# A cap on bulk weight loads in flight, and Wo loaded in four pieces, in a fused attention and MLP block

## The chip, the cores and the metric

The kernel runs on one core of one Trainium2 chip. A core has TensorE (PE, matmuls), VectorE (DVE), ScalarE (ACT, activation functions), GpSimd (POOL) and SyncE (SP), which here only issues DMAs. Each engine runs its own instructions in order and waits on semaphores for the others. The metric is the device time of one execution in microseconds (us); the median of three runs counts.

## The reference

One transformer block in bfloat16 for 2048 tokens: layer norm, attention with 32 heads of 32, an output projection with a residual, layer norm, and an MLP with tanh-GELU and a second residual.

```python
# x [1, 2048, 1024]; wqkv [1024, 3072]; wo [1024, 1024]; w1 [1024, 3584]; w2 [3584, 1024]
def A(x):                       # H = 32, Dh = 32
    q, k, v = heads(x @ wqkv)
    p = softmax(q @ k.T * Dh ** -0.5)
    return merge(p @ v) @ wo
def B(x):
    return gelu_tanh(x @ w1 + b1) @ w2 + b2
h = x + A(layernorm(x))
out = h + B(layernorm(h))       # layernorm: (x - mean) / sqrt(var + 1e-5), no weights
```

## The kernel before

**Order by a planner.** The kernel does not write its instructions down directly. `Graph.add` (L96) records tasks with their engine, an assumed duration, a priority, and the tasks that they depend on, found from the buffers that each reads and writes. `Graph.schedule` (L119) then plays the whole program through in simulated time and fixes the order of each engine's tasks. On SP it takes, of the tasks that are ready, the one of lowest priority number, and of these the one recorded first. It counts on 280 GB/s for all DMAs together, one after the other, and a fixed latency of 2.1 us. There are 24 lanes, a semaphore each, for DMAs in flight; a DMA waits for the one before it on its lane. `assign` (L229) turns dependencies into semaphore waits, and `emit` (L322) writes the order out. So an edit of the planner's DMA rules can move matmuls and vector work too: the order on all engines follows from its simulated times. On the chip that order is fixed, and only the semaphores decide when each instruction runs.

**Stages.** Norm, transposes and the first projections start the kernel (about 25 us). From then on attention runs as 512 rounds: a group of eight score matmuls (`Att.qk`, L805) writes two units of two PSUM banks, and two exponentials of 128 x 1024 (L816) empty them into PT or, at the start, PX buffers. PV matmuls (L842) and softmax sums (L857 on DVE, L871 on PE) follow. Three units of PSUM rotate, so ScalarE is at most one exponential ahead of the next group of scores. A unit of queries is 256 tokens, u = 0 to 7. Between the score groups the planner fits the remaining TensorE work in ("bg"): projections, and for each unit u the output projection `wo(u)`, the norm `ln2(u)`, `ffn1(u)` and `ffn2(u, j)` for the two halves j of the output columns. For unit 7 these can only follow the last exponential: they form a serial end. `pick_pe` prefers scores, and it may put idle matmuls ("keep") where nothing else is ready in two stretches (`KEEP`).

**Weights.** `block_copies` (L909) first rewrites Wo, W1 and W2 in HBM as contiguous blocks of 512 KB (Wo: two of 1 MB), at priority 3. After that every unit loads all of them again, since they don't fit beside the attention buffers. SBUF has a ring of four 512 KB slots for W1 (`a_w1r`) and one of seven for W2 (`a_w2r`); unit 7's FFN1 and FFN2's second half have rings of their own where K and V lay (`b_w1r`, `b_w2r`, which share their space). Wo (`wov`, two tensors of 1 MB) lies over the four W1 slots: `wo(u)` needs slots 0 and 1 for its first 1 MB and slots 2 and 3 for its second. All these loads have priority 1. A load is issued when its slot's last reader is done, so the loads for the next unit's first half of W2 go out as soon as slots come free, far ahead of their use, and there is no limit on how many are in flight.

Other DMAs on SP's queue: query tiles QT (64 KB, priority -1), query scratch writes, residual rows `hch`, output rows, and the DMA transposes of the normed rows (`hnT`, priority -1), on which FFN1 depends.

Names in the profile: `w_blocks` and `wo_blocks` are the HBM blocks, `gT` the MLP's hidden layer, `OT` attention's output, `uu` the GELU's temporary (its Tanh is L1023). All DMAs carry L589, the matmul helper L565 (four narrow tiles) and L568 or L571 (one whole).

Of the kernel before, what the change touches and what calls it, by code (L numbers as in the profile page):

```python
# [10 lines left out]
E = mybir.EngineType  # L11

P = 128
# [4 lines left out]
KEEP = ((262, 298), (930, 1010),)  # L18
KEEP_COLS = 512
KEEP_GAP = -0.08  # L20


class Buf:
# [42 lines left out]
class Graph:  # L66
# [47 lines left out]
    def schedule(self, pick_pe, pool, switch=0.104, dma_rate=280.0, dma_lat=2.1, dma_issue=0.06):  # L114
# [9 lines left out]
        state = {"mode": None, "dma": 0.0}  # L124
        events = []
        n = 0
        num = {t: i for i, t in enumerate(self.tasks)}

        def release(t):
# [16 lines left out]
        while n < total:  # L146
# [5 lines left out]
            now = heapq.heappop(events)  # L152
            while events and events[0] <= now + 1e-9:
                heapq.heappop(events)
            for e in self.ENGS:
                while free[e] <= now + 1e-9:
                    up = upcoming[e]
                    rd = ready[e]
# [4 lines left out]
                    if e == E.PE:  # L163
                        state["next"] = up[0][0] if up else None
                        t = pick_pe(rd, now, state, free_banks(now))
                    else:
                        t = min(rd, key=lambda x: (x.prio, num[x]))
                        if up and t.prio > 0:

                            for (rt, _, u) in up[:6]:  # L170
                                if u.prio < t.prio and rt < now + 0.6 * t.occ:
                                    t = None
                                    break
# [3 lines left out]
                    if t.acq is not None:  # L177
                        b = min([x for x in free_banks(now) if x in t.acq.banks], key=lambda x: max([y.done for y in pool[x]], default=0.0))
# [8 lines left out]
                    t.order = len(seqs[e])  # L187
                    seqs[e].append(t)
                    if e == E.SP:
                        k = min(range(self.n_lanes), key=lambda i: lanes[i].done if lanes[i] else 0.0)  # L190
                        if lanes[k] is not None:
                            t.deps.add(lanes[k])
                            start = max(start, lanes[k].done)
                        lanes[k] = t
                        t.lane = k
                        free[e] = start + dma_issue
                        s0 = max(state["dma"], start + 0.9)
                        state["dma"] = s0 + t.bytes / dma_rate / 1e3
                        t.done = max(state["dma"], s0) + dma_lat - 0.9
                    else:  # L200
                        free[e] = start + t.occ
                        t.done = start + t.occ + t.lat
# [135 lines left out]
def build_kernel(nc, A_x, A_wqkv, A_wo, B_w1, B_b1, B_w2, B_b2, out):  # L338
# [7 lines left out]
    DC = D // P  # L346
# [237 lines left out]
    def dma(out_ap, in_ap, nbytes, reads=(), writes=(), prio=0, noncontig=False, after=()):  # L584
        def fn(s):
            if noncontig:
                with nc.allow_non_contiguous_dma(reason="strided gather"):
                    return s.dma_start(out_ap, in_ap)
            return s.dma_start(out_ap, in_ap)  # L589
        return gr.add(E.SP, fn, 0.06, 0.0, reads, writes, prio, nbytes=nbytes, after=after)  # L590
# [350 lines left out]
    def wo(u, tail=False):  # L941
        R = R1
        nb = 0
        R.cnt["w1"] += -R.cnt["w1"] % 4
        for j in range(2):
            dma(wov[j][:, :, :], wod[j], P * DC * 1024, reads=[B_wod[j]], writes=R.B_w1[2 * j:2 * j + 2], prio=1)
        R.cnt["w1"] += 4
        for t in range(2):
            hs = 2 * (u % 2) + t
# [2 lines left out]
            for j in range(2):  # L952
# [4 lines left out]
                order = range(G) if tail else [7, 0, 1, 2, 3, 4, 5, 6]  # L957
                for k, g in enumerate(order):
                    mm(bank, OT[:, u % 3, g, t * P:(t + 1) * P], wov[j][:, g, :], k == 0, k == 7 and not tail,
                       [B_OT[u % 3][g][t], R.B_w1[s], R.B_w1[s + 1]], not tail)  # L960
                if tail:
                    mm(bank, ident[:, :], hch[:, hs, c], False, True, [B_ident, B_hch[hs][j]], False)
                    act(lambda a, hs=hs, c=c, bank=bank: a.activation(hch[:, hs, c], psum[:, bank, :], ACT.Copy), 512,
# [63 lines left out]
    def ffn2(u, j, wide=False, W=None, banks=None):  # L1027
# [3 lines left out]
        ws = []  # L1031
        for q in range(FC // 4):
            s = W.next("w2", W.nw2)
            dma(W.w2[:, s, :, :], w2d[j, q], P * 4096, reads=[B_w2d[j][q]], writes=[W.B_w2[s]], prio=1)
            ws.append(s)
        for t in range(2):
            bank = banks[t] if banks and banks[t] is not None else slot()
# [302 lines left out]
```

## Time and profile before

| | |
|---|---|
| median of three runs | 1080.27 us (1079.21 to 1081.98) |
| the profiled execution | 1079.06 us |
| its span, first to last instruction | 1077.3 us, at full granted TensorE clock |
| DMA engines | moved 196.37 MB, 182 GB/s on average; busy for 54.0% with the data queue, 0.9% with the "instruction" queue |
| W2 blocks `a_w2r` | 105 loads of 512 KB, median 5.2 us from issue to landing |
| W1 blocks `a_w1r` | 98 loads of 512 KB, 3.5 us |
| Wo `wov` | 16 loads of 1 MB, 4.8 us |
| DMA transposes `hnT` | 14, median 3.2 us |

A line of a group names the source line, the engine, the operation, what it writes and reads, and how often; then its busy time, the mean of one in ns, and the engine's idle time just before it with what ended most of that. A line of the chain or of the timeline has the start in us, the duration, the engine or line, and how many instructions are merged; a bracket tells idle time before it and what ended it. A line of the waits has the waiting engine and line, whom it waited for, and total us, times, longest. An exponential lasts longer (1084 ns in the median) than the distance between two, since ScalarE overlaps them.

### The profile page before, as it was taken

Reading aid. Unit: us, or ns where it says so; the run is one execution under the profiler, and the core shown is the slowest. Engines: PE = TensorE matmul, PEld = TensorE weight load, DVE = VectorE, ACT = ScalarE, POOL = GpSimd, SP = SyncE. Lnnn points to the kernel's source line nnn. Section 1 sums busy time; section 2 is a strip of 40 time slices with the busy share of each in tenths; the row PEclk is TensorE's granted clock in tenths of the full one; section 3 lists DMA queues with packets and bytes.
Section 4 is the critical chain, followed back from the end, with each engine's and each line's share of the span. In section 5 each row is a group of like instructions: output and inputs, shape, how many; then the busy total and the mean of one; then the engine's idle time right before and its main releaser. Section 6 shows DMA issues by size and latency. Waiting matters only on the chain.

```text
span 1077.3 us, 41835 instructions
## 1 busy us (share of the span) xinstructions
PE 1053.3 (98%) x19071; PEld 609.4 (57%) x19071; DVE 747.3 (69%) x1438; ACT 1013.3 (94%) x1116; POOL 45.4 (4%) x110
## 2 busy tenths in 40 slices
PE   8999999999999999999999999999999999999998
PEld 6576555554444754674475457447545754575483
DVE  8776666566576895698489659948975976696401
ACT  4999999999999999999999999999999999999650
POOL 4200000000010000001000100100010000000100
PEclk9999999999999999999999999999999999999999
DMA  8561543438473555655664764466375555866260
GB/s 223 166 172 30 159 134 119 138 119 297 165 186 130 188 191 181 232 181 169 217 240 164 209 230 179 154 223 230 144 232 205 186 200 181 294 220 250 94 244 19
DMA packets 136177, 196.37 MB, mean 182 GB/s; under 512 B 49216, under 2 KB 100288, under 8 KB 133184
## 3 DMA queue, kind: packets, MB, share of 16 engines
q1 hardware_dynamic: 136000, 193.70, 54.0%
q8 instruction: 149, 2.44, 0.9%
q14 instruction: 28, 0.23, 0.1%
HBM read 177.94 MB, written 27.26 MB: 190 GB/s over the span
## 4 chain that ended last, share of the span: by engine, by line
ACT 60%; PE 33%; DVE 4%; POOL 1%; issue 1%; DMA 0%; SPq 0%; POOLq 0%; DVEq 0%
ACT PT L816 55%; PE ps L568 11%; PE ps L565 7%; PE ps L571 5%; PE ps L805 5%; PE ps L842 3%; ACT PX L816 3%; ACT uu L1023 2%; PE ps L871 2%; DVE PS L857 1%; DVE st L617 1%; DMA xrb<-in_A_x_dram 0%; DVE gT L1001 0%; DVE gT L1025 0%; POOL denb L626 0%
## 5 line engine op out<-in xcount | busy, mean ns | idle before, releaser
L816 ACT ACTIVATE PT<-ps 128x1024 bf16<-128x1024 f32 x992 | 922.0, 1094 | 5.9 <-PE ps L805 5.7
L857 DVE TENSOR_TENSOR PS<-PT 128x1024 bf16<-128x1024 bf16 x431 | 285.3, 685 | 132.4 <-PE ps L871 67.6
L805 PE MATMUL ps<-QT,KT 32*128 32x256 bf16 x4096 | 203.9, 273 | 5.6 <-ACT PT L816 2.7
L842 PE MATMUL ps<-PT,V 128*32 128x256 bf16 x3968 | 174.2, 273 | 2.1 <-ACT PT L816 1.7
L805 PEld LDWEIGHTS ps<-QT,KT 32*128 32x128 bf16 x4096 | 61.0, 92 | 161.4 <-ACT PT L816 135.9
L871 PE MATMUL ps<-PS,ones 128*32 128x256 bf16 x1756 | 122.0, 274 | 2.3 <-DVE PS L857 1.2
L842 PEld LDWEIGHTS ps<-PT,V 128*32 128x32 bf16 x3968 | 101.7, 97 | 28.5 <-issue 7.0
L568 PE MATMUL ps<-hnT,a_w1r 128*128 128x256 bf16 x940 | 114.5, 273 | 0.6 <-DVE gT L1001 0.5
L565 PE MATMUL ps<-a_w2r,gT 128*32 128x512 bf16 x1436 | 102.2, 381 | 0.1
L568 PEld LDWEIGHTS ps<-hnT,a_w1r 128*128 128x128 bf16 x940 | 86.8, 98 | 24.4 <-issue 13.7
L568 PE MATMUL ps<-a_w2r,gT 128*128 128x512 bf16 x397 | 97.6, 381 | 0.8 <-DVE hch L966 0.6
L565 PE MATMUL ps<-hnT,a_w1r 128*32 128x256 bf16 x2512 | 89.8, 274 | 3.5 <-DVE OD L894 1.5
L1001 DVE TENSOR_TENSOR gT<-ps,b1f 128x512 bf16<-128x512 f32 x98 | 67.3, 686 | 16.0 <-PE ps L568 8.0
L565 PEld LDWEIGHTS ps<-hnT,a_w1r 128*32 128x32 bf16 x2512 | 61.8, 96 | 19.5 <-issue 16.5
L1046 DVE SCALAR_TENSOR_TENSOR hch<-ps,hch 128x512 bf16<-128x512 f32 x32 | 21.9, 685 | 70.5 <-PE ps L571 47.1
L871 PEld LDWEIGHTS ps<-PS,ones 128*32 128x32 bf16 x1756 | 46.2, 96 | 26.6 <-DVE PS L857 8.6
L568 PEld LDWEIGHTS ps<-a_w2r,gT 128*128 128x128 bf16 x397 | 33.7, 98 | 46.5 <-issue 13.0
L568 PE MATMUL ps<-xnT,Wall 128*128 128x512 bf16 (+1 forms) x272 | 57.4, 346 | 0.4 <-ACT xnT L645 0.2
L1023 ACT ACTIVATE uu<-uu 128x1024 bf16<-128x1024 bf16 x49 | 54.3, 1113 | 0.0
L565 PEld LDWEIGHTS ps<-a_w2r,gT 128*32 128x32 bf16 x1436 | 32.0, 96 | 25.4 <-issue 13.5
L622 POOL CAST mvb<-mv 128x2 bf16<-128x2 f32 (+1 forms) x25 | 5.2, 216 | 972.5 <-DVE mv L619 972.5
L568 PE MATMUL ps<-wov,OT 128*128 128x512 bf16 x146 | 35.4, 380 | 1.4 <-DVE OD L894 0.8
(93 smaller groups left out, 1020.8 us busy)
## 6 DMA issues: line engine op xcount, KB each, us to landing
a_w2r<-w_blocks SPq DMA_DIRECT2D x105, 512.0 KB, 5.2
a_w1r<-w_blocks SPq DMA_DIRECT2D x98, 512.0 KB, 3.5
wov<-wo_blocks SPq DMA_DIRECT2D x16, 1024.0 KB, 4.8
w_blocks<-in_B_w_dram SPq DMA_DIRECT2D x28, 512.0 KB, 3.9
b_w1r<-w_blocks SPq DMA_DIRECT2D x14, 512.0 KB, 3.9
a_w1r<-in_A_wqkv_dram SPq DMA_DIRECT2D x11, 512.0 KB, 5.5
Wall<-in_A_wqkv_dram SPq DMA_DIRECT2D x17, 256.0 KB, 4.9
xrb<-in_A_x_dram SPq DMA_DIRECT2D x16, 256.0 KB, 4.7
```

What stands on the lines that cost most here:

```text
L565: fns.append(lambda p, j=j: p.matmul(psum[32 * j:32 * j + 32, bi(bank), c0:c1], lhsT[:, 32 * j:32 * j + 32], rhs, start=start, stop=stop, ...
L568: t.whole = lambda p: p.matmul(psum[:, bi(bank), c0:c1], lhsT, rhs, start=start, stop=stop, skip_group_check=True)
L571: t = pe(lambda p: p.matmul(psum[:, bi(bank), c0:c1], lhsT, rhs, start=start, stop=stop), occ, reads=reads, writes=[bb(bank)], mode="full" ...
L617: dve(lambda v, c=c, k=k, x_ap=x_ap: v.bn_stats(st_l[:, i + k, 6 * c:6 * c + 6], x_ap[:, 512 * c:512 * c + 512]), 0.595, reads=B_x if isin ...
L805: return p.matmul(psum[:, 2 * us[h // 2] + h % 2, 256 * i:256 * i + 256], KT[32 * h:32 * h + 32, g, k0:k0 + P], QT[32 * h:32 * h + 32, qs, :],
L816: act(lambda a, u=u, k=k: a.activation(PTs[s][:, k, :, :], psum[:, 2 * u:2 * u + 2, :], ACT.Exp, bias=0.0, scale=SCALE), 1024, reads=[B_ps ...
L842: fns.append(lambda p, i=i, h=h: p.matmul(psum[32 * h:32 * h + 32, bi(bank), 0:256], V[:, g, 2 * r + i, 32 * h:32 * h + 32], PTs[s][:, h / ...
L857: dve(lambda v: v.tensor_tensor(PS[:, n, :, :], pairs[:, :, 0:256], pairs[:, :, 256:512], ALU.add), c_dve(1024, 2), reads=B_PTs[s], writes ...
L871: fns.append(lambda p, h=h, rhs=rhs, i=i: p.matmul(psum[32 * h:32 * h + 32, bi(bank), 256:512], ones32[:, :], rhs, start=False, stop=last, ...
L1001: t = dve(lambda v: v.tensor_tensor(g[:, fc:fc + 2, :], psum[:, bi(bank), :].rearrange("p (f c) -> p f c", f=2), b1f[:, fc:fc + 2].unsquee ...
L1023: act(lambda a: a.activation(w, w, ACT.Tanh, bias=0.0, scale=KT2), 1024, reads=[B_uu[i]], writes=[B_uu[i]], prio=-1)
L1046: drop(dve(lambda v, hs=hs, bank=bank, half=half: v.scalar_tensor_tensor(hch[:, hs, c], psum[:, bi(bank), :], half, hch[:, hs, c], ALU.mul ...
```

## The change

- The planner keeps a list of bulk loads: DMAs of 512 KB or more with priority 1 or 2. Such a load may be issued only when the loads before it that are still out, with itself, are no more than three units of 512 KB (priority 1) or two (priority 2). The wait for the earlier landing becomes a semaphore wait in the program.
- For bulk loads the planner counts on 350 GB/s instead of 280.
- The first half of W2 (j = 0) has priority 2 instead of 1: where both are ready, W1, Wo and the second half of W2 go first.
- Wo comes in four loads of 512 KB instead of two of 1 MB, each into one W1 slot, and each Wo matmul waits only for the piece that it reads.

The writes of normed rows to scratch early in the kernel (1 MB, priority 1) fall under the limit too; the HBM-to-HBM copies (priority 3) and the reloads of Wqkv (priority 0 and below) don't.

```diff
+BULK = {1: 3, 2: 2}
+UNIT = 1 << 19
...
+        bulk = []
+
+        def behind(t):
+            k = BULK[t.prio] - t.bytes // UNIT
+            for b in reversed(bulk):
+                k -= b.bytes // UNIT
+                if k < 0:
+                    return b
+            return None
...
-                        t = min(rd, key=lambda x: (x.prio, num[x]))
+                        go = rd
+                        if e == E.SP:
+                            go = []
+                            for x in rd:
+                                b = behind(x) if x.bytes >= UNIT and x.prio in BULK else None
+                                if b is None or b.done <= now + 1e-9:
+                                    go.append(x)
+                                else:
+                                    heapq.heappush(events, b.done)
+                            if not go:
+                                break
+                        t = min(go, key=lambda x: (x.prio, num[x]))
...
+                        if t.bytes >= UNIT and t.prio in BULK:
+                            b = behind(t)
+                            if b is not None:
+                                t.deps.add(b)
+                            bulk.append(t)
...
-                        state["dma"] = s0 + t.bytes / dma_rate / 1e3
+                        state["dma"] = s0 + t.bytes / (350.0 if t.bytes >= UNIT and t.prio in BULK else dma_rate) / 1e3
...
         for j in range(2):
-            dma(wov[j][:, :, :], wod[j], P * DC * 1024, reads=[B_wod[j]], writes=R.B_w1[2 * j:2 * j + 2], prio=1)
+            for i in range(2):
+                dma(wov[j][:, 4 * i:4 * i + 4, :], wod[j][:, 4 * i:4 * i + 4, :], P * DC * 512, reads=[B_wod[j]],
+                    writes=[R.B_w1[2 * j + i]], prio=1)
...
-                       [B_OT[u % 3][g][t], R.B_w1[s], R.B_w1[s + 1]], not tail)
+                       [B_OT[u % 3][g][t], R.B_w1[s + g // 4]], not tail)
...
-            dma(W.w2[:, s, :, :], w2d[j, q], P * 4096, reads=[B_w2d[j][q]], writes=[W.B_w2[s]], prio=1)
+            dma(W.w2[:, s, :, :], w2d[j, q], P * 4096, reads=[B_w2d[j][q]], writes=[W.B_w2[s]], prio=2 if j == 0 else 1)
```

In the built program SP issues 480 DMAs instead of 464. TensorE's score matmuls, and the work of DVE, ACT and POOL, keep their number; their order among each other changes in many places between the start and the last exponential. The narrow and whole forms of the other matmuls are mixed a little differently, and there are 31 idle matmuls instead of 24.

## The prediction

> **What bounds the kernel now.** I read the page first: busy shares, the costliest groups, the DMA issues.
>
> ```profile
> span 1077.3 us, 41835 instructions
> ...
> PE 1053.3 (98%) x19071; PEld 609.4 (57%) x19071; DVE 747.3 (69%) x1438; ACT 1013.3 (94%) x1116; POOL 45.4 (4%) x110
> ...
> L816 ACT ACTIVATE PT<-ps 128x1024 bf16<-128x1024 f32 x992 | 922.0, 1094 | 5.9 <-PE ps L805 5.7
> ...
> a_w2r<-w_blocks SPq DMA_DIRECT2D x105, 512.0 KB, 5.2
> a_w1r<-w_blocks SPq DMA_DIRECT2D x98, 512.0 KB, 3.5
> wov<-wo_blocks SPq DMA_DIRECT2D x16, 1024.0 KB, 4.8
> ```
>
> TensorE and ScalarE are both nearly full, so the question is which sets the pace. The chain of waits, in order of time, shows long runs of exponentials (L816) back to back:
>
> ```profile
> 64.09 251.43 ACT PT L816 x274
> ...
> 492.41 57.00 ACT PT L816 x62
> 549.41 0.94 ACT uu L1023
> ```
>
> 251.43 / 274 = 0.9176 us for one exponential when nothing holds it up; a Tanh (L1023) is 0.94. Line 816 has 1024 executions (992 into PT, 32 into PX), two of them before 21.82 us. From the start of the third at 21.82 to the start of the last at 1009.69 there are 987.87 us. The work in them is 1021 x 0.9176 + 49 x 0.94 = 982.9. So ScalarE loses 4.9 us in 988, and this is all that a change between these two points can win. The list of waits agrees:
>
> ```profile
> ACT PT L816 <- PE ps L805: 5.7, 8, 3.0
> ```
>
> Eight gaps make 5.7 us, and the longest, 3.0, lies in the start-up before 21.82; the other seven make 2.7, and the rest of the 4.9 is slips too short to be listed. I looked at the seven in the timeline. The largest two are like this one, at 425 us:
>
> ```profile
> 424.77 0.28 PE L805 MATMUL ps<-QT,KT 32*128 32x256 bf16 x1
> ...
> 425.54 0.39 PE L805 MATMUL ps<-QT,KT 32*128 32x256 bf16 x7 [0.49 <-issue]
> ...
> 425.98 1.94 ACT L816 ACTIVATE PT<-ps 128x1024 bf16<-128x1024 f32 x2 [0.62 <-PE ps L805]
> ```
>
> TensorE stops inside a group of score matmuls, waiting for nothing that the profile shows, and the next exponential starts 0.62 late (0.77 of delay, so the reserve here is 0.15). Four of the seven are of this kind: 0.62, 0.26, 0.19 and 0.82 us of ScalarE idle at 425, 738, 808 and 925, together 1.89. In all four a 16 KB packet of the queue that the page calls "instruction" starts 2.2 to 2.3 us before the stall ends; I take them for code that arrives late, an inference. The other three (0.16, 0.44, 0.18 at 362, 757, 907) are places where TensorE had more work than the exponentials gave it time for. None of the seven waits for a weight load. The load with the least time to spare is Wo's second megabyte:
>
> ```profile
> 485.47 0.32 SPq L589 DMA_DIRECT2D wov<-wo_blocks  x1
> ...
> 492.00 1.25 PE L568 MATMUL ps<-wov,OT 128*128 128x512 bf16 x5
> ```
>
> It lands 4.7 us after its issue, at 490.15, and its first matmul starts at 492.00: 1.85 to spare.
>
> After the last exponential comes a serial end: the last Wo, its norm, FFN1 and FFN2.
>
> ```profile
> 1025.57 24.63 PE L571 MATMUL ps<-hnT,b_w1r 128*128 128x256 bf16 x224
> 1027.52 10.80 SPq L589 DMA_DIRECT2D b_w2r<-w_blocks  x7
> 1050.03 12.25 PE L571 MATMUL ps<-a_w2r,gT 128*128 128x512 bf16 x56
> 1062.12 12.25 PE L571 MATMUL ps<-b_w2r,gT 128*128 128x512 bf16 x56
> ```
>
> 1010.81 to 1077.3 is 66.5 us of TensorE and norm work, with the loads ahead of it.
>
> **The change, part by part.**
>
> *Start-up.* The order on every engine up to the exponentials at about 45 us is the same; then V and K projections trade places by at most 0.65 us before a transposed tile is used. The tiles had 0.3 to 3 us to spare there, and the tightest one keeps its place: 0.
>
> *Serial end.* In the changed program the instructions of TensorE after the last score matmul stand in the same order and number, and ScalarE's too. What moves is a load: with first-half W2 behind second-half W2, the last two blocks of a_w2r are issued after the seven b_w2r loads. Those are released by FFN1's matmuls, one every 24.63 / 14 = 1.76 us, as before (10.80 for seven, until 1038.3). Two more loads then take 0.4 of issue and at most the 6.7 us of the slowest weight load looked at (the one issued at 441.93): landed by 1045.5. They are needed for blocks 5 and 6, 20 matmuls of 0.219 after 1050.03, at 1054.4. Cost 0; without that cover each microsecond late would be one on the end.
>
> *Wo in four pieces.* 16 issues become 32: 16 x 0.32 = 5 us more of SP's queue over the run, which has free stretches of that size in each stage (492.4 to 496.1 is one). A piece starts when its own 512 KB slot is free. In exchange the planner starts Wo's matmuls sooner. I counted, in the built order, the exponentials between the matmul that frees a slot and the first matmul that reads the piece, times 0.9176. For the old 1 MB load the count gives 6.6 us at the place above, where the trace has 6.53. For the new pieces the shortest of each stage from wo(1) to wo(5) are 5.5, 4.1, 4.5, 5.2 and 4.9. A 512 KB load with little beside it lands in 3.1 to 3.5; the piece before it is issued some 2 us earlier or more, and loads in a train finish 1.26 us apart (those issued from 512.57 to 514.68, 416 GB/s). So 3.1 to 4.4, and 0 to 1.0 us to spare in the tightest: cost 0. If landing took the busy median 5.2, three of the stages would be late by 1.1, 0.7 and 0.3, less 0.15 each: 1.7 in all.
>
> *The limit.* SP now also waits for an earlier landing. Behind the waiting load stand score operands (QT), output rows, norm rows and the transposes. QT has over 100 us to spare from wo(1) on, the hnT transposes 25 to 41 but for the last one (5.9, after a landing of 7.8), so a wait of 1 to 2 us costs nothing there. By the same count every other 512 KB load that follows wo(0) keeps at least 6.5 us from issue to use, against 10.6 before for second-half W2 (5.5 landing, 5.1 to spare), and 3 in flight at 1.26 us each need 3.3 to 5. Cost 0. First-half W2 had some 54 us to spare and may go last.
>
> *What it can win.* Most of all the burst at 885 to 920, where over a dozen loads stood in the queue, the transpose issued at 918.88 took 7.8 us to land instead of 2.7, and the largest gap (0.82) follows. No row shows a code fetch with the bulk limited. Bounds: 0, if fetches don't mind bulk, and -1.89, if all four gaps go. The fetch packets took 1.05 us on average with no weight load outstanding, 0.99 with one, 1.03 with two, 1.09 with three: nearly blind to the load. I take -0.5, near the end that this row is near. The page "DMA: Bandwidth & Descriptors" of the Trainium skill, section "Queues, rings and completion order", says that each DMA engine serves its queue rows in turn, a packet at a time; by that a fetch never stands behind the whole bulk, the term would be 0 and the time 1080.3. The packet times agree with it; how long a fetch waits before its packet starts no run here shows.
>
> *The new order.* ScalarE's order has the same 49 Tanh at other places, with one pair of Tanh back to back as before; the three gaps of 0.78 us from overfull places come back elsewhere: 0, between -0.78 and +1.5 (three or four more such places at 0.4).
>
> **Sum.** 1077.3 of span and 1.8 around it make 1079.06 for the profiled run, 1.2 under the median of the three, 1080.27. The change is 0 + 0 + 0 + 0 - 0.5 + 0: 1078.6 on the profiled run, 1079.8 on the median, which I predict.
>
> **Rivals.** Times are against 1080.27; 0.3%, about what a measurement of this kernel can tell from no change, is 3.2 us.
> 1. *The limit hardly acts, or acts and the code fetches don't mind*: slots come free one by one, so rarely are more than three loads out. For it: FFN1's loads are issued 2 to 3 us apart and land in 3 to 5. Against: the bursts at 434 and 509. Then nothing moves: 1080.3.
> 2. *Faster*: bulk in the queue is behind the short slips as well as the gaps, and nearly all of the 4.9 goes: 1080.27 - 4.2 = 1076.0. For it: the burst at 900; against: the slips also lie before 225 us, where few weight loads run.
> 3. *Slower by landing*: TensorE runs in order, so a late Wo piece holds up the score matmuls behind it. If the last piece took the 6.7 us of the busiest load, five stages would be late by 1.2, 2.6, 2.2, 1.5 and 1.8, less 0.15 each: +8.6, 1088.9. It decides from landings of some 5.6 on. For it: the planner now counts on 350 GB/s for bulk; against: trains here reached 416.
> 4. *Slower by order*: the moved matmuls overfill more rounds, eight or more at 0.4: 1083.7.
>
> **Chances.** Forecast 0.40, rival 1 0.16, rival 2 0.16, rival 3 0.18, rival 4 0.10. Faster by over 0.3%: 0.16; within: 0.56; slower: 0.28. The range 1075.0 to 1086.5 takes in rivals 2 and 4 and the nearer half of rival 3; without the rivals on either side it would be 1077.9 to 1082.
>
> **What would show it.** Right: exponentials from 21.8 to about 1009 us with some 4 us lost, the same 66.5 us after the last, seven or so gaps with fewer of the "issue" kind, a median landing of a_w2r nearer 3.5 than 5.2, and no wait of TensorE for a wov or weight load. Wrong: TensorE idle ended by a DMA into wov or a_w2r (rival 3), a ScalarE loss under 2 us (rival 2), or a serial end that isn't 66.5 us.

## The result, and the profile after

| | median us | runs | ratio to before, 95% interval |
|---|---|---|---|
| before | 1080.27 (1078.74 to 1081.98) | 11 | |
| changed | 1086.62 (1081.39 to 1089.22) | 11 | 1.0054 [1.0037, 1.0070] |
| changed, measured again | 1083.83 (1080.88 to 1087.42) | 10 | 1.0033 [1.0014, 1.0051] |

The change makes the kernel 3.5 to 6.4 us slower; the prediction was 1079.8, with 1086.5 as the upper end of its range. (The lines that the text above gives for the planner's functions are off by a few: in the kernel before, `add` is at L89, `schedule` L114, `assign` L234, `emit` L327 and `block_copies` L918.)

The profiled run took 1087.34 us. Its page, with L816 now L846, L805 now L835, L565 and L568 now L595 and L598:

```profile
span 1085.5 us, 41815 instructions
...
PE 1046.6 (96%) x18983; PEld 611.8 (56%) x19048; DVE 748.7 (69%) x1438; ACT 1014.3 (93%) x1116; POOL 45.5 (4%) x110
...
L846 ACT ACTIVATE PT<-ps 128x1024 bf16<-128x1024 f32 x992 | 922.0, 1077 | 12.5 <-PE ps L835 12.2
...
a_w2r<-w_blocks SPq DMA_DIRECT2D x105, 512.0 KB, 4.9
a_w1r<-w_blocks SPq DMA_DIRECT2D x98, 512.0 KB, 3.9
wov<-wo_blocks SPq DMA_DIRECT2D x32, 512.0 KB, 4.1
```

The exponentials' own work is the same 922.0, but ScalarE now idles 12.5 us ahead of them instead of 5.9. Counted as in the prediction, the third exponential starts at 22.41 (0.6 later), 12.6 us are lost between it and the last instead of 4.9, and 66.5 us follow, as before: 0.6 + 7.6 + 0.0 is the 8.2 by which the span grew. The loads hardly land sooner: W2 in 4.9 instead of 5.2, and W1 later, in 3.9 instead of 3.5.

Nine gaps delay an exponential by over 0.25 us, together 10.7; before there were seven, together 3.8. The three largest are in this timeline:

```profile
736.99 0.50 PE L595 MATMUL ps<-hnT,a_w1r 128*32 128x256 bf16 x12
...
739.73 0.40 PE L595 MATMUL ps<-hnT,a_w1r 128*32 128x256 bf16 x8 [2.24 <-issue]
...
740.51 1.02 ACT L846 ACTIVATE PT<-ps 128x1024 bf16<-128x1024 f32 x1 [2.26 <-PE ps L835]
...
922.44 0.32 SPq L619 DMA_DIRECT2D b_w1r<-w_blocks  x1
922.81 1.26 SPq L624 DMA_TRANSPOSE hnT<-a_xb  x1
...
928.42 1.24 SPq L624 DMA_TRANSPOSE hnT<-a_xb  x1
...
934.51 1.05 PE L595 MATMUL ps<-hnT,a_w1r 128*32 128x256 bf16 x16 [2.30 <-DMA hnT<-a_xb]
...
937.86 1.94 ACT L846 ACTIVATE PT<-ps 128x1024 bf16<-128x1024 f32 x2 [3.38 <-PE ps L835]
...
970.92 0.82 PE L595 MATMUL ps<-hnT,a_w1r 128*32 128x256 bf16 x23
973.35 1.70 PE L595 MATMUL ps<-hnT,a_w1r 128*32 128x256 bf16 x53 [1.61 <-issue]
...
975.44 1.02 ACT L846 ACTIVATE PT<-ps 128x1024 bf16<-128x1024 f32 x1 [1.78 <-PE ps L835]
```

Two stalls of the "issue" kind, in which TensorE stops inside a group of FFN1 matmuls and a fetch packet has started 2.4 us before the stall ends, leave ScalarE idle for 2.26 and 1.78 us. The third is a real wait: the second transpose for unit 6's FFN1, issued at 928.42, lands 5.95 us later, the matmul that reads it is next in TensorE's order, and ScalarE idles 3.38. Behind this wait the TensorE clock falls in this profile. In the view by stretches (length, then busy time of each engine, then the granted clock, DMA share, GB/s):

```profile
926.00:930.00 4.00, 3.45 (x48) 1.17 (x49) 2.63 (x6) 4.00 (x6) 1.09 (x2) 1.00 0.97 315
930.00:934.00 4.00, 2.06 (x34) 0.65 (x30) 0.69 (x1) 4.00 (x5) 0.00 (x0) 0.94 1.22 241
934.00:938.00 4.00, 3.49 (x64) 2.35 (x68) 0.69 (x1) 0.62 (x2) 0.00 (x0) 0.50 0.25 95
938.00:942.00 4.00, 3.89 (x60) 2.24 (x52) 2.49 (x7) 3.56 (x4) 0.00 (x0) 0.70 0.37 125
```

After four microseconds at 52% busy the clock is 0.50 for some 7 us, from 933.5 on. A group of 24 narrow matmuls, 0.83 us at full clock, takes 1.52 there. The wait doesn't always bring this. In run e17 below, which has the same order up to here, it is as long and the clock stays at 1.00 (a line of its timeline, then one of its stretches):

```profile
934.88 0.62 PE L595 MATMUL ps<-hnT,a_w1r 128*32 128x256 bf16 x16 [2.32 <-DMA hnT<-a_xb]
...
934.00:938.00 4.00, 2.97 (x96) 2.19 (x96) 1.05 (x2) 2.07 (x3) 0.00 (x0) 1.00 0.42 147
```

There the next exponential is 2.26 late. Here it is 3.72 late, and another one 0.54 right behind it: the drop of the clock cost some 2 us more.

### The profile page after: what moved, and what is told of

It reads as the page before. It is cut to its first block, busy times and chain, and to the rows that moved or that the text cites. A ratio compares the mean times of both kernels' runs of the same rounds, so it can differ in the third digit from the quotient of the medians.

```text
span 1085.5 us, 41815 instructions
## 1 busy us (share of the span) xinstructions
PE 1046.6 (96%) x18983; PEld 611.8 (56%) x19048; DVE 748.7 (69%) x1438; ACT 1014.3 (93%) x1116; POOL 45.5 (4%) x110
## 4 chain that ended last, share of the span: by engine, by line
ACT 58%; PE 36%; DVE 3%; DMA 1%; issue 1%; POOL 0%; SPq 0%; POOLq 0%; DVEq 0%
ACT PT L846 53%; PE ps L598 11%; PE ps L595 9%; PE ps L601 5%; PE ps L835 5%; PE ps L872 4%; ACT PX L846 3%; PE ps L901 2%; ACT uu L1055 2%; DVE st L647 1%; DMA hnT<-a_xb 1%; DMA xrb<-in_A_x_dram 1%; DVE PS L887 0%; DMA wov<-wo_blocks 0%; DVE gT L1033 0%
## 5 line engine op out<-in xcount | busy, mean ns | idle before, releaser
L846 ACT ACTIVATE PT<-ps 128x1024 bf16<-128x1024 f32 x992 | 922.0, 1077 | 12.5 <-PE ps L835 12.2
L835 PE MATMUL ps<-QT,KT 32*128 32x256 bf16 x4096 | 203.8, 273 | 5.3 <-ACT PT L846 3.5
L835 PEld LDWEIGHTS ps<-QT,KT 32*128 32x128 bf16 x4096 | 60.8, 92 | 159.7 <-ACT PT L846 129.1
L598 PE MATMUL ps<-hnT,a_w1r 128*128 128x256 bf16 x965 | 118.7, 273 | 0.4 <-issue 0.3
L598 PEld LDWEIGHTS ps<-hnT,a_w1r 128*128 128x128 bf16 x965 | 88.3, 98 | 26.3 <-issue 14.7
L595 PE MATMUL ps<-a_w2r,gT 128*32 128x512 bf16 x1376 | 98.7, 381 | 1.4 <-DVE gT L1057 0.6
L598 PE MATMUL ps<-a_w2r,gT 128*128 128x512 bf16 x389 | 95.0, 380 | 3.9 <-issue 2.5
L595 PE MATMUL ps<-hnT,a_w1r 128*32 128x256 bf16 x2412 | 87.9, 277 | 10.6 <-issue 4.3
L1033 DVE TENSOR_TENSOR gT<-ps,b1f 128x512 bf16<-128x512 f32 x98 | 67.3, 687 | 21.7 <-PE ps L595 12.6
L595 PEld LDWEIGHTS ps<-hnT,a_w1r 128*32 128x32 bf16 x2412 | 60.7, 97 | 26.2 <-issue 22.7
L598 PEld LDWEIGHTS ps<-a_w2r,gT 128*128 128x128 bf16 x412 | 35.5, 98 | 48.3 <-issue 11.4
L598 PE MATMUL ps<-xnT,Wall 128*128 128x512 bf16 (+1 forms) x279 | 59.3, 347 | 2.0 <-issue 1.1
L595 PEld LDWEIGHTS ps<-a_w2r,gT 128*32 128x32 bf16 x1376 | 30.0, 96 | 27.1 <-issue 14.1
L598 PEld LDWEIGHTS ps<-xnT,Wall 128*128 128x128 bf16 x296 | 25.3, 98 | 26.2 <-issue 7.6
```

Of the source, the lines that this page charges most:

```text
L595: fns.append(lambda p, j=j: p.matmul(psum[32 * j:32 * j + 32, bi(bank), c0:c1], lhsT[:, 32 * j:32 * j + 32], rhs, start=start, stop=stop, ...
L598: t.whole = lambda p: p.matmul(psum[:, bi(bank), c0:c1], lhsT, rhs, start=start, stop=stop, skip_group_check=True)
L835: return p.matmul(psum[:, 2 * us[h // 2] + h % 2, 256 * i:256 * i + 256], KT[32 * h:32 * h + 32, g, k0:k0 + P], QT[32 * h:32 * h + 32, qs, :],
L846: act(lambda a, u=u, k=k: a.activation(PTs[s][:, k, :, :], psum[:, 2 * u:2 * u + 2, :], ACT.Exp, bias=0.0, scale=SCALE), 1024, reads=[B_ps ...
L1033: t = dve(lambda v: v.tensor_tensor(g[:, fc:fc + 2, :], psum[:, bi(bank), :].rearrange("p (f c) -> p f c", f=2), b1f[:, fc:fc + 2].unsquee ...
```

## The experiments

All ratios are against the kernel before, run on the same chip in the same call. "Lost" is the time lost between the third and the last exponential, "issue" the part of it in gaps over 0.25 us that a TensorE stall called issue makes, with a fetch packet that started 2.1 to 2.6 us before the stall ends; both from one profile each. That profile is of the first run, not of a typical one: e13's is its slowest run (1085.75), e15's its fastest (1078.62). (For the kernel before that is five gaps; the fifth, at 755, the prediction had counted among the overfull rounds.)

| run | median us | ratio, 95% interval | lost | issue |
|---|---|---|---|---|
| before | 1080.27 | | 4.9 | 3.1 |
| changed | 1086.62 | 1.0054 [1.0037, 1.0070] | 12.6 | 5.4 |
| e1 changed again | 1083.83 | 1.0033 [1.0014, 1.0051] | 8.1 | 5.2 |
| e2 its order, no limit on the chip | 1080.10 | 0.9997 [0.9978, 1.0016] | 3.9 | 0.5 |
| e3 order of before, with limit | 1081.63 | 1.0016 [0.9999, 1.0033] | 6.8 | 5.0 |
| e4 transposes counted later | 1081.48 | 1.0007 [0.9989, 1.0025] | 7.6 | 5.3 |
| e5 limit 2 and 1 | 1137.64 | 1.0537 [1.0513, 1.0561] | 61.9 | |
| e6 no limit around unit 6's transposes | 1083.55 | 1.0035 [1.0024, 1.0046] | 6.4 | 3.6 |
| e7 before, small W2 loads | 1078.11 | 0.9983 [0.9968, 0.9997] | 2.5 | 0.5 |
| e8 pieces alone | 1078.20 | 0.9986 [0.9976, 0.9996] | 3.3 | 1.0 |
| e9 changed, small W2 loads | 1080.67 | 1.0005 [0.9990, 1.0019] | 4.6 | 2.3 |
| e10 limit 4 and 3 | 1081.67 | 1.0011 [0.9995, 1.0026] | 6.3 | 3.0 |
| e11 pieces' order, with limit | 1077.77 | 0.9973 [0.9962, 0.9984] | 3.5 | 2.4 |
| e12 pieces alone again | 1078.47 | 0.9979 [0.9969, 0.9990] | 4.8 | 1.8 |
| e13 changed, 280 GB/s assumed | 1081.01 | 1.0002 [0.9985, 1.0019] | 8.3 | 4.0 |
| e14 changed, one priority | 1083.79 | 1.0026 [1.0008, 1.0044] | 6.0 | 3.4 |
| e15 pieces, 350 GB/s assumed, no limit | 1081.02 | 0.9999 [0.9981, 1.0017] | 4.0 | 1.2 |
| e16 changed, Wo in 1 MB loads | 1081.28 | 1.0006 [0.9990, 1.0022] | 5.4 | 2.7 |
| e17 changed, more idle matmuls | 1086.21 | 1.0044 [1.0031, 1.0057] | 11.1 | 5.0 |
| e18 before, more idle matmuls | 1080.41 | 0.9991 [0.9981, 1.0001] | 4.9 | 2.9 |

**Order or waits?** The first four runs take the change apart: the planner's order on one side, the waits on the other.

e1, the changed kernel unaltered:

> The changed kernel once more, unaltered: which of its gaps come back? Theory A (the planner's new order starts unit 6's FFN1 right behind a transpose that lands late, and a dip of the granted clock follows): the gap of some 3.4 us of ScalarE's idle time near 933 us, ended by score matmuls behind a wait on hnT, is there again, and the granted clock is again below 1.000. Theory B (code fetches that come late): gaps with a TensorE stall called issue, 2.26 at 737 and 1.78 at 972 in the first profile, come back at the same places if the order of the code causes them, and elsewhere or not at all if they are chance. Time 1084 to 1088 by either; under 1083 would say that chance makes most of the loss.

e2:

```diff
                             b = behind(t)
-                            if b is not None:
-                                t.deps.add(b)
                             bulk.append(t)
```

> The changed order of every engine, but without the semaphore waits on earlier landings that the limit puts on SP: the planner still counts with the limit, the chip does not. Theory A (order): the gap near 933 stays, since FFN1 still stands right behind the transpose, and with more loads in flight the transpose lands no earlier; 1085 to 1088. Theory C (the waits themselves hold loads back and cost SP some 0.3 us each): loads land earlier before their use, PE's waits for wov, a_w2r and a_w1r go, and the time is 1080 to 1083.

e3, in the kernel before, at the end of `schedule`:

```diff
+        for t in seqs[E.SP]:
+            if t.bytes >= UNIT and t.prio in BULK and t.kind != "first":
+                self.behind(t, 3, bulk)
+            elif t.bytes >= UNIT and t.kind == "first":
+                self.behind(t, 2, bulk)
```

> The order of the kernel before on every engine, with Wo in two pieces of 1 MB as before, and the limit only as semaphore waits on the earlier landings (3 units, 2 for first-half W2). Theory A: the order makes the loss, so this is 1080 to 1082 with the granted clock at 1.000. Theory C: the waits make it, so 1083 to 1088. If limiting the bulk helped the code fetches, as the prediction had it, 1078 to 1080 and fewer issue stalls than the four of the kernel before.

e4:

```diff
-                        t.done = max(state["dma"], s0) + dma_lat - 0.9
+                        t.done = max(state["dma"], s0) + dma_lat - 0.9 + (2.5 if t.kind == "tr" else 0.0)
```

> The changed kernel, but the planner counts on 2.5 us more for the landing of the hnT transposes (about 6.1 from the issue, where the last one took 5.95). SP's order stays; the other engines differ only from unit 6's norm on. Theory A: the gap near 933 shrinks from 3.4 to under 1 us and the dip of the clock with it, so 1082 to 1084 and a clock of 1.000 in most runs. Theory B or C: the place matters little, 1085 to 1088.

The changed order without the waits takes 1080.1, as theory C had it (though TensorE still waits once for a Wo piece, 0.94 of delay at 773): theory A, as it was put, fell. It wanted the gap near 933 to stay in e2. In e2's timeline no exponential is late there:

```profile
912.52 23.10 ACT L844 ACTIVATE PT<-ps 128x1024 bf16<-128x1024 f32 x25
...
915.72 1.24 SPq L622 DMA_TRANSPOSE hnT<-a_xb  x1
...
925.90 1.59 SPq L622 DMA_TRANSPOSE hnT<-a_xb  x1
...
929.62 0.62 PE L593 MATMUL ps<-hnT,a_w1r 128*32 128x256 bf16 x16
```

25 exponentials run in one piece. The first transpose goes out at 915.72, against 922.81 (919.06 in e1), where SP first waits with a load of b_w1r (until 922.44); with the waits taken from these loads alone, in e6 below, it goes out at 917.22. The loads around it go out together, and the last of them lands at 926.4, half a us after the second one is issued: it lands in 2.86 us instead of 5.95 (e1: 5.55), 0.86 ahead of its first matmul. In the changed kernel three weight loads are out when it is issued, until 929.4, 930.6 and 933.5. So the limit didn't keep bulk out of the way; it stretched the same bulk over the time of the second transpose.

The time of e1, 1083.8, is just under the 1084 to 1088 that either theory gave. In e1 the gaps near 931 and 968 came back (1.84 and 1.91 of delay), and so they did in e17 (2.26 and 1.94). The gap at 737 came back in e17 (1.87) and in e4, but not in e1. The second is the same instruction every time, first in e1, then in e17:

```profile
966.03 0.83 PE L595 MATMUL ps<-hnT,a_w1r 128*32 128x256 bf16 x23
968.48 1.70 PE L595 MATMUL ps<-hnT,a_w1r 128*32 128x256 bf16 x53 [1.62 <-issue]
```

```profile
969.06 0.82 PE L595 MATMUL ps<-hnT,a_w1r 128*32 128x256 bf16 x23
971.54 1.70 PE L595 MATMUL ps<-hnT,a_w1r 128*32 128x256 bf16 x53 [1.65 <-issue]
```

So an issue stall isn't chance alone. It takes a late fetch: in e1 the packet starts 2.36 us before the stall ends, in e2, with the same order, 4.1 us before TensorE gets to the same instruction, and the 76 matmuls of this group run in one piece. That it also takes a dense stretch of code is likely and not shown: from 900 to 980 us the changed order has 492 narrow FFN1 matmuls, the order of before 256.

e4 moved FFN1 away from the transpose, and both gaps are gone (2.3 to 5.1 us less than the changed kernel), with the same 5.3 of issue gaps elsewhere. It was expected at 1082 to 1084 with a clock of 1.000 in most runs; it came out a little better, with the lower clock in 6 of 10. e3 lies in the range of theory A, with an interval that touches 1; its order is that of before, and its issue gaps rose from 3.1 to 5.0. It also shows by itself how long the limit can hold SP. The last transpose of unit 6 before (the first line), then SP in e3, and the first matmul of e3 that reads the transpose:

```profile
918.88 2.67 SPq L594 DMA_TRANSPOSE hnT<-a_xb  x1
...
920.70 3.83 SPq L606 DMA_DIRECT2D a_w2r<-w_blocks  x3
924.58 0.42 SPq L606 DMA_DIRECT2D b_w1r<-w_blocks  x1
929.53 0.32 SPq L606 DMA_DIRECT2D a_w2r<-w_blocks  x1
929.90 1.24 SPq L611 DMA_TRANSPOSE hnT<-a_xb  x1
...
934.58 0.93 PE L585 MATMUL ps<-hnT,a_w1r 128*128 128x256 bf16 x7
```

SP waits for landings until 920.70 and again until 929.53, so the transpose goes out 11 us later. It lands at 934.47. Of the 5.9 us that it had to spare before, 0.1 are left.

**How much limit?** e5 and e10 have the changed order, and the limit as waits only, with other numbers of units; e6 leaves the waits out on SP's DMAs 404 to 429.

```diff
-            if b is not None:
+            if b is not None and not 404 <= t.order <= 429:
```

> The changed order of every engine as in the run without waits (which took 1080.1), with a stricter limit put in as waits: 2 units (1 for first-half W2) where the change has 3 and 2. Theory C (the waits spread the loads in time, so that urgent small transfers and code fetches find two or three loads out nearly always, and loads land late): more of the same, 1086 to 1092, with PE's waits for wov, a_w2r or a_w1r among the gaps. Theory D (what hurts is three 512 KB loads out at once when a transpose or a code fetch comes, and a tighter limit relieves them): 1079 to 1083, shorter landings of hnT and fewer issue stalls.

> The changed kernel with its limit everywhere but on the 17 weight loads that SP issues between 898 and 939 us, ahead of and around the transposes of unit 6 (same order on all engines). Theory C with its main place here: these loads go out early and in one burst as in the run without waits, the first transpose is issued near 916 instead of 919 to 923, the last lands near 929, the gap of 1.8 to 3.7 at 931 to 933 goes, and the time is 1080.5 to 1082.5. If the loss is spread over all stages instead: 1083 to 1086.

> The changed order as in the run without waits, with a looser limit put in as waits: 4 units, 3 for first-half W2. With no limit this order took 1080.1, with 3 and 2 units 1083.8 to 1086.6, with 2 and 1 units 1137.6. Theory C: between the first two, 1080 to 1083, and the gap before unit 6's FFN1 smaller than 1.8 us. If any wait on landings costs the same, 1083.5 or more.

With no limit, 4 and 3, 3 and 2, 2 and 1 units the same order takes 1080.1, 1081.7, 1083.8 to 1086.6 and 1137.6. Theory D fell: at 2 and 1 a W2 load lands in 3.7 us instead of 4.9, and still many loads come too late. The list of waits of e5 has

```profile
ACT PT L856 <- PE ps L845: 60.0, 22, 10.7
PE ps L605 <- DMA a_w1r<-w_blocks: 19.5, 4, 6.0
...
PE ps L605 <- DMA hnT<-a_xb: 9.6, 1, 9.6
```

e6 missed: the gap near 932 shrank to 0.8 and the one near 968 to 0.4, and the first transpose went out at 917.2, about as expected, but the last landed at 932.0 instead of near 929, and the time is 1083.55, not 1080.5 to 1082.5. Its profile has issue gaps of 1.6 and 1.4 near 455 and 555; e1 has the first of them (1.4), e2 neither. The limit's cost isn't in one place.

**Traffic or semaphores?** e7 and e9 shrink the W2 loads, once without and once with the limit:

```diff
-            dma(W.w2[:, s, :, :], w2d[j, q], P * 4096, ...)
+            n, m = (4, 512) if u == 0 and j == 0 or W is not R1 else (1, 256)
+            dma(W.w2[:, s, 0:n, 0:m], w2d[j, q][:, 0:n, 0:m], P * 4096, ...)
```

> The kernel before, same order of every engine and same number of DMAs, but every load of a_w2r after the first seven moves 32 KB of the 512 KB: FFN2 from unit 0's second half on, but for unit 7's second half, is computed from incomplete W2 blocks. It asks what the traffic itself costs through late code fetches. Theory F (the time from the point where TensorE has used up enough code to the start of the fetch packet grows with the loads that are out: mean 1.9, 2.0, 2.5, 3.1, 3.6 us with 0, 1, 2, 3, 4 loads in the trace of before): hardly any fetch finds over two loads out, the issue gaps fall from 5 (2.9 us of delay) to 2 or fewer, and the time to 1077 to 1078.5. If the fetches are late because TensorE runs through dense code there, the gaps stay and the time is 1080.

> The changed kernel with limit and order, but every load of a_w2r after the first seven moves 32 KB of 512 KB (FFN2 but for unit 0's first half and unit 7's second half is computed from incomplete W2 blocks). Four profiles with the limit so far (the changed kernel twice, the limit on the order of before, the later transposes) show 5.0 to 5.4 us of delay in issue gaps, four without it or with smaller traffic 0.5 to 3.1. Theory F (with the limit, two or three loads are out for 49% of the time instead of 32 to 37%, and code fetches wait behind them): with the traffic gone the waits are short, the issue gaps fall under 2 us and the time to 1078 to 1081. Theory S (the semaphore waits on SP themselves, not the traffic): 1083 or more.

Less traffic takes 1.9 us from the kernel before and leaves one issue gap of 0.5; from the changed kernel it takes 3 to 6. Both times are those of theory F, but e9 keeps two issue gaps (0.6, and 1.7 at 965, again the x53 group), 2.3 together where theory F said under 2. And not all that e9 wins is code fetches: its transposes for unit 6 also land in time. With W2's traffic gone on both sides the changed kernel is still 2.4 us behind (1.0005 against 0.9983). So W2's traffic makes a part of the loss, and not all.

**Which part of the change?**

e8 and e12, the kernel before with the hunk on Wo's four loads and the matmuls' reads, nothing else:

> The kernel before with only Wo in four pieces, each into its own slot: no limit, no change of priority or of the assumed rate (the planner orders anew). The prediction costed this part at nothing: 1079.5 to 1081.5. If late pieces matter even without the limit (they landed in 3.5 to 5.0 us in the changed kernel, with nothing to spare at 382, 482 and 571 us): 1082 to 1084 and PE's waits for wov among the gaps.

> Wo in four pieces alone once more, unaltered: it took 1078.2 against 1080.0, a ratio of 0.9986 with an interval that just leaves out 1. If that is a gain, the interval leaves out 1 again at 1077.5 to 1079.3, and the profile again has some 3.3 us lost between the third and the last exponential against 4.9 before. If it was chance, 1079.5 to 1081.

e11, the order of e8, with the waits of e3:

> The order of the kernel with Wo in four pieces alone (1078.2), and the limit of 3 and 2 units as semaphore waits only. Theory C or F: 1080 to 1084, over 1.5 us above the pieces alone, with more issue gaps than the one of 1 us there. If the limit costs only together with the order that the planner makes for it: 1078 to 1079.5.

e13 to e16, one part undone each (e15: e8 with the rate):

```diff
e13:  -  (350.0 if t.bytes >= UNIT and t.prio in BULK else dma_rate)
      +  dma_rate
e14:  -  BULK = {1: 3, 2: 2}      prio=2 if j == 0 else 1
      +  BULK = {1: 3}            prio=1
e15:  -  state["dma"] = s0 + t.bytes / dma_rate / 1e3
      +  state["dma"] = s0 + t.bytes / (350.0 if t.bytes >= UNIT and t.prio == 1 else dma_rate) / 1e3
e16:  the two 1 MB loads of Wo and their reads as in the kernel before
```

> The changed kernel with one number back: the planner counts on 280 GB/s for bulk loads again (limit, priorities and Wo pieces stay). Theory G (the planner's promise: with 350 GB/s it believes the last transpose of unit 6 landed at 924.6 in its own time, with 280 at 925.8, in the kernel before and with the pieces alone at 927.1 to 927.2, and it places unit 6's FFN1 0.1 us behind that belief; the real landing then has nothing to spare): the gap near 931 falls to about 1 us or less, and the time to 1078 to 1081. If the limit itself makes the loss in an order that is planned with it: 1083 or more.

> The changed kernel without the lower priority and the tighter limit for first-half W2 (all weight loads: 3 units, priority 1). Theory G: the rate is still 350 and the belief still 924.6, so the gap near 931 and the one near 966 stay: 1082 to 1086. If the priority makes the loss: 1078 to 1080.

> Wo in pieces and the assumed rate of 350 GB/s, but no limit and one priority: the planner's belief for the last transpose is 924.6 as in the changed kernel, and no load waits for another on the chip. Pieces alone took 1078.2 and 1078.5, the changed order without waits 1080.1. Theory G alone: the rate costs 1.5 to 3 by itself, 1079.5 to 1081.5. If rate and limit hurt only together: 1077.5 to 1079.3.

> The changed kernel with Wo in two loads of 1 MB as before (limit, priorities and rate stay). The pieces alone gained 1.8; without them, if the parts add up, this is 1.5 to 2 above the changed kernel's 1083.8 to 1086.6: 1085 to 1088. If the pieces, which then land with nothing to spare, make the loss under the limit: 1080 to 1083.

The pieces alone are a gain, small and twice measured: 1078.2 and 1078.5, both intervals below 1. Where the gain lies the profiles don't say: e12 lost 4.8, not the 3.3 of e8 that was expected again. With the limit as waits on top (e11) they are as fast, 1077.8, the best of all runs. Its page:

```profile
L833 ACT ACTIVATE PT<-ps 128x1024 bf16<-128x1024 f32 x992 | 921.0, 1090 | 5.2 <-PE ps L822 4.9
```

Theories C and F, in the strong form that the limit always costs, fell with it: this order, planned at 280 GB/s and with no limit in the plan, bears the limit. Its issue gaps did grow (2.4, against 1.0 and 1.8 with the pieces alone), but its last transpose for unit 6 lands 2.6 us before its use. In the changed order that is 0.9 even without the limit (e2).

The assumed rate costs something by itself. Pieces with 350 instead of 280 have a ratio of 0.9999 instead of 0.9986 and 0.9979, without any limit: 1.4 to 2.2 us, with intervals that overlap a little, and with the lower clock (below) in 8 of 10 runs instead of 2 of 22. The changed kernel with 280 takes 1081.0 instead of 1083.8 to 1086.6; in its profile the gap at 931 is gone, and the last transpose lands 1.4 us before its use. It isn't everything, since e13 is still 3 us above e11.

Undoing the priority changes nothing that shows in the time (e14: 1083.8), but its profile contradicts theory G: the belief is still 924.6, and yet the last transpose lands 0.3 us before its use and no gap is left near 931. The gap near 968 is there (1.72), and with issue gaps of 3.4 in all the kernel is as slow as e1. So the transpose alone doesn't explain the loss. In e16 the first expectation missed and the second held: without the pieces the changed kernel isn't slower but faster, 1081.3, about as much as with the rate undone. So the parts don't add up. Each of them makes the planner deal out a new order; which of these orders the limit hurts, and by how much, is settled for the place at 931 only.

**The clock.** The last two runs add six idle matmuls:

```diff
-KEEP = ((262, 298), (930, 1010),)
+KEEP = ((262, 298), (930, 1023),)
```

> The changed kernel with six idle matmuls added among the last seconds of attention: the second KEEP stretch ends at exponential 1023 instead of 1010 (nothing else moves). In the changed order, and in that of before, TensorE is busy for 0.84, 0.54 and 0.6 of the last three stretches of 2 us ahead of the last exponential, with the pieces alone 1.00, 0.73 and 0.52, and runs with a mean granted clock under 1.000 are 16 of 21, 17 of 31 and 2 of 22, each some 2 us longer than the others. Theory K (the clock dips at the start of the serial end because of the light stretch ahead of it): few runs under 1.000, and 1082 to 1084 instead of 1083.8 to 1086.6. If the dips come from elsewhere: 1084 to 1087, most runs under 1.000.

> The kernel before with the same six idle matmuls at the end of attention. Theory K: hardly a run under a mean clock of 1.000 (17 of 31 for the kernel before), and 1079 to 1079.7 against 1080.3. If the dips don't depend on the light stretch, or the idle matmuls delay scores: 1080 to 1081.5.

The reason is this stretch of e2, whose last exponential starts at 1009.3:

```profile
1005.30:1007.30 2.00, 1.09 (x24) 0.34 (x20) 0.93 (x2) 2.00 (x3) 0.00 (x0) 1.00 0.03 8
1007.30:1009.30 2.00, 1.29 (x21) 0.48 (x22) 0.86 (x2) 2.00 (x3) 0.00 (x0) 0.70 0.11 20
1009.30:1011.30 2.00, 2.00 (x8) 0.40 (x8) 0.01 (x1) 1.11 (x2) 0.00 (x0) 0.50 0.66 242
```

TensorE works 1.09 and 1.29 of 2 us in many short pieces, no pause over 0.5, and the clock halves for some 7 us at the start of the serial end: 69.3 us from the last exponential to the end instead of 66.5. The kernel before has the same light stretch, and 77 of its 135 runs with the experiments had a mean granted clock under 1.000; their medians are 1.2 to 2.1 us above those of the others in the same call. With the pieces the stretch is shorter, in e8:

```profile
1004.10:1006.10 2.00, 1.47 (x40) 0.51 (x28) 0.88 (x2) 2.00 (x3) 0.00 (x0) 1.00 0.20 66
1006.10:1008.10 2.00, 1.03 (x23) 0.45 (x22) 0.93 (x2) 2.00 (x4) 0.00 (x0) 1.00 0.00 0
```

and 5 of 32 runs of e8, e11 and e12 had the lower clock. e18 fills it,

```profile
1005.90:1007.90 2.00, 2.00 (x31) 0.63 (x23) 0.93 (x2) 2.00 (x3) 0.00 (x0) 1.00 0.02 4
1007.90:1009.90 2.00, 1.84 (x24) 0.55 (x23) 0.80 (x2) 2.00 (x4) 0.00 (x0) 1.00 0.19 25
```

and 1 of 12 runs had the lower clock, against 10 of 17 of the kernel before in that call: the light stretch is the cause of the dips there. What it is worth is 0.9991 [0.9981, 1.0001], at most 2 us and not safely told from nothing. e17 missed: it was expected at 1082 to 1084 with few dips and took 1086.2, with the lower clock in 3 of 6 runs, and 1084.9 to 1085.5 in the three others. The main loss of the change isn't the clock.

## Why the prediction was wrong

**What bounds the kernel: right.** ScalarE's pace sets the time up to the last exponential, 66.5 us follow, and all that moved is time lost between exponentials.

**Start-up and serial end: right** but for 0.6 us at the start, where 0 was said; the last 66.5 us are unchanged, with W2's last blocks in time.

**Wo in four pieces, "cost 0": the term was off, by a gain.** The landings, sized at 3.1 to 4.4, came out at 3.5 to 5.0 from wo(1) on, and the tightest pieces (issued at 482, 573 and 766 us) had 0.1 to 0.2 to spare. That cost at most 0.5 in one gap (at 488). The part as a whole won 1.5 to 2.3 us, for a reason that the prediction didn't look at: of it, some 0.7, an estimate, is the clock (57% against 16% of runs with the dip, at some 1.7 each), the rest isn't located.

**The limit, "a wait of 1 to 2 us costs nothing there. ... Cost 0": this is the step that failed.** On the changed order the waits cost 3.7 to 6.5 us (e2 against e1 and the changed kernel). Two things make up most of it, the wait for the transpose and the code fetches of the next paragraph. In the profiles, from e2 to e1 and to the changed kernel, the issue gaps grew by 4.7 and 4.9, and the gaps behind the transpose added 1.8 and 4.3. So the fetches are the larger part, and the transpose is the largest single loss.

The step took the spare time of the transposes and loads from the trace of before, the last hnT with 5.9, and put waits of 1 to 2 us against it. Both terms were wrong. The waits are longer: in e3, with the order of before, the limit alone sent this transpose out 11 us later, and in the changed order the first one of unit 6 went out 3 to 7 us later than in e2, the second into company. And the spare time was no reserve that a new plan keeps. The planner sets unit 6's FFN1 some 0.1 us behind the time at which it believes that the last transpose landed: 927.1 of its own time before, 924.6 with 350 GB/s. On the chip FFN1 started at 932.6 before, since the plan as a whole runs ahead of the chip (it ends at 1071.6, where the chip takes 1077.3). Most of the 5.9 was this lead. In the new plan the belief is 2.5 earlier, while the landing is 2.0 later even without the limit (928.8 in e2 against 926.7), and 0.9 was left. The prediction had named the very transpose.

**Code fetches, "I take -0.5": wrong in sign, and the second step that failed.** The gaps of this kind grew from 3.1 to 5.4 us. With the same order on both sides, without and with the limit, they went from 3.1 to 5.0 (e3), from 0.5 to 5.2 and 5.4 (e2 against e1 and the changed kernel) and from 1.0 and 1.8 to 2.4 (e8 and e12 against e11). In the ten profiles with three units and full traffic they come to 2.4 to 5.4 us, mean 4.2; in the six without a limit to 0.5 to 3.1, mean 1.75.

The row used was how long a fetch packet takes (about 1.05 us whatever the load), which is blind to load; the prediction said itself that no run shows how long a fetch waits before its packet starts. The trace of before does show it. TensorE's instructions come in blocks of 256, one 16 KB packet each. All five issue gaps end at an instruction whose number, counted over all of TensorE's in the trace, is 193 to 195 over a multiple of 256, so one can count how far TensorE had come when the packet started. From a count of 150 over such a multiple the packet came after 1.9, 2.1, 2.5, 2.9 and 3.8 us on average, with 0, 1, 2, 3 and 4 weight loads out at that count (60, 46, 23, 11 and 8 packets; the expectation of e7 has another count of the loads). The limit cuts off the bursts (four or more loads out for 6.4% of the time from 300 to 1000 us before, 0 after) but keeps two or three out longer (49% instead of 32%), and the mean lateness of all fetches didn't fall: 2.2 before, 2.1 in e1. Why the late ones hit dense code more often is open.

The Trainium skill's page "Runtime: NRT & Kernel Launch", section "Instruction fetch mechanics", says that code is fetched in 16 KB blocks of 256 instructions while the ones before run, and that this is mostly hidden. The blocks agree with the trace; on narrow matmuls here it isn't hidden, up to 2.24 us of a stall at one boundary.

**The new order, 0, between -0.78 and +1.5: right by chance.** e2, which has the new order and the pieces, lies at -0.2. But the pieces alone won 1.5 to 2.3 and the assumed rate on top of them lost 1.4 to 2.2: two terms that the prediction put at 0 cancel.

**Rivals.** The one for slower by landing had the right side and the wrong tile: it asked for Wo pieces of 5.6 us and over, and they landed in 5.0 at most; the tile that came late was hnT. The limit did act, against the first rival. The one for slower by order foresaw neither the clock nor the fetches. Faster (1076.0) was reached by no run: e7, with W2's loads shrunk, got to 1078.1, and e11, with another order, to 1077.8.

## What to carry to other kernels

Where a planner places the work, spare time in the old trace is no reserve for a change of the planner's numbers: look up what the new plan believes and how far behind that belief it puts the first reader, and let it be pessimistic. A limit on transfers in flight spreads them: here small urgent transfers met as many loads as before, or more, and with an in-order issuing queue the limit also delayed whatever stood behind a held load, by up to 11 us. Holding the bulk back for the urgent transfers alone would be another change; no run here tries it. When several parts are changed at once, measure each alone: here one part was worth 0.2% and was hidden by the others.

## What the runs showed of the hardware

- The TensorE clock halves (0.50) in light stretches without any long pause: in e2 no pause ahead of the drop is over 0.41 us. The Trainium skill's page "TensorE: Matmul & The Clock Gate", section "HAM oscillation — how this bites in real kernels", puts the rule as no idle gaps over some 3.4 us, and the throttled rate as 4/8; the rate agrees with the 0.50 here, the rule doesn't, since shorter pauses were enough.
- The drops fall on a grid. Leaving out those at the program's end, the 20 profiles have 17 drops, each a whole number of steps of 3.41 us after the clock's first rise (271 steps in the changed kernel, 293 in e2, 295 in e1), and each lasts one, two or three steps. In the step ahead of each, TensorE was busy for at most 60%; other steps as light passed without a drop (57% around the wait in e17). So a light stretch stood ahead of every drop and isn't enough by itself, and the grid may be why the same kernel drops in some runs and not in others. Six idle matmuls of 0.4 us took the dips from 10 of 17 runs to 1 of 12.
- A DMA transpose lands in 2.7 us alone and in up to 8.3 beside weight loads (e15). With a limit of three loads the slowest took 4.6 (e3), 6.5 (e1) and 8.2 (e14), against 7.8 before.
- A code fetch that starts late stops TensorE for up to 2.24 us (in the changed kernel at 737), and at the same instruction in several runs (near 968 in e1 and e17).
